# Two attention pairs transposed on TensorE, four output tiles in a borrowed buffer, one clear dropped, and later load estimates in a statically planned transformer kernel

## The chip, the cores and the metric

The kernel runs on one core of one Trainium2 chip. The metric is the device time of one execution in microseconds (us), the median of several executions. Each execution also reports its span (first to last instruction, about 1.7 us less than the device time) and the mean granted clock of TensorE, as a share of full speed. PE is TensorE, DVE is VectorE, ACT is ScalarE, POOL is GpSimd, SP is the engine that issues most DMAs.

## The reference, cut to what matters

Four layers follow each other on a sequence of 2048 tokens of width 640, in bf16: attention with a compressive memory, a feed-forward layer, then the same two again, each behind a layer norm and with a residual.

```python
x = x + A(layernorm(x))      # 32 heads of 20, 4 segments of 512 tokens
x = x + B(layernorm(x))      # relu(x @ w1) @ w2, inner width 1728
x = x + A(layernorm(x))
x = x + B(layernorm(x))
# A, per segment s: causal softmax attention inside the segment,
# and for s > 0 a read of the memory M, z that the earlier segments wrote
```

## The kernel before

The kernel does not issue instructions in the order of its source. Every stage is a generator that yields operations with an estimated cost; a list scheduler in the kernel orders them for the five engines and puts in semaphores. It does so 20 times, each time with due times worked out from the plan before, and emits the plan with the smallest estimated end:

```python
for n in range(PLANS):                      # PLANS = 20
    P, S = plan(dues)
    end = max(S.t.values())
    if best is None or end < best[0]:
        best = (end, P, S)
    dues = justify(S, dues, n)
```

Each engine gets its instructions in the planned order. Where an estimate is wrong, an instruction that is ready stands behind one that is not (3.67 us in the case near 305 us below). The planner also puts some useless "filler" matmuls on PE (`ps<-ident`, 50 in the kernel before).

The heads are laid out in groups of four, on partition rows 0-19, 32-51, 64-83 and 96-115. Three of the eight head groups (tile `kqL`) are made by a relay. In the first segment a set of selector matmuls does it; later segments go through DRAM:

```python
def relay_pe(a, s):                         # RELAY_PE = (0,): first segment only
    sel = hT[:, 0:128 * len(pieces)]...     # selectors, lent room in hT
    tz = yield dve(..., lambda e: e.memset(sel, 0.0))
    for i, (m, c, d0, d1) in enumerate(pieces):
        ... e.tensor_copy(selector slots, ident slots)        # seven small DVE copies
    # ... PE: matmul(bank, sel[:, i], kq chunk); evacuation to kqL[:, n, m, :], all 128 partitions
```

GpSimd clears `kqL` once at the start, and the relay waits for that:

```python
KQL[0].take()
def consts():
    # ...
    tl = yield pool(1600.0, lambda e: e.memset(kqL[:], 0.0))   # 3072 columns of bf16
    KQL[0].drop(tl)
    tm = yield pool(400.0, lambda e: e.memset(maskg[:], 0.0))
```

The results of an attention pair (two head groups) are evacuated (copied out of PE's result bank) to `oraw` and turned by one DMA transpose, then divided by the softmax sum on DVE:

```python
def turn(n, a, s, g, od, tk):
    # ... x == 0: evacuate to oraw[:, 0]; x == 1: to oraw[:, 1]
    tx, ok = yield XK(rw, [t0, te])                             # DMA transpose of the pair
    tr, rd = yield dve(240, 1, lambda e, d: e.reciprocal(d, ov[:, :, :, DH:E1]), [tx], [RDEN])
    # ... two products into o_sb
```

The output tiles of the first segment are then transposed on PE into two slots of `oT` (`OT`), and the output projection reads them.

The softmax here doesn't subtract the row's maximum and nothing guards it: scores larger than these inputs give would overflow.

Of the kernel before, what the change touches and what calls it, by code (L numbers as in the profile page):

```python
# [7 lines left out]
ACT = mybir.ActivationFunctionType  # L8
# [488 lines left out]
def bass_interleave_layers__memory_aug_infini_attn__dense_activation_relu__prompt_kernel(  # L497
    nc, A_x, A_wq, A_wk, A_wv, A_wo, A_beta, B_x, B_w1, B_w2, out,
):
    with contextlib.ExitStack() as es:  # L500
# [3 lines left out]
        def sem_(name):  # L504
            if name not in sems:
                sems[name] = es.enter_context(nc.semaphore(name))
            return sems[name]
# [4 lines left out]
        LN2_APART = (0, 7)  # L512

        LN1_PE, LN2_PE, OT_PE = (0, 1), (0,), (0,)
        HALVES = (0,)
        RELAY_PE = (0,)
        NXT, NXN, NET = 3, 2, 2
        wq_p = sb("wq_p", [128, FC, D])
        wk_p = sb("wk_p", [128, FC, D])
# [48 lines left out]
        def plan(dues):  # L568
# [22 lines left out]
            RMEM = [Slot(rmem[:, k], "rmem") for k in range(2)]  # L591
            OT = [Slot(oT[:, k], "oT") for k in range(2)]
            HT = [Slot(hT, "hT")]
            xnt_sem = [[sem_("xt%d_%d" % (k, i)) for i in range(NJ)] for k in range(NXT)]
            scw_sem = [[sem_("sw%d_%d" % (b, r)) for r in range(4)] for b in range(2)]
            scr_sem = [sem_("sr%d" % r) for r in range(4)]
# [14 lines left out]



            def ld(e, name, nbytes, fn, key, waits=(), issue=700.0, lat=2600.0):
                tk = yield dma(e, sem_("d_" + name), nbytes, fn, waits, issue=issue, lat=lat, rate=380.0)
                S.set(*key, v=[tk])
                return tk
# [93 lines left out]
                zb = yield dve(320, 1, lambda e: e.memset(w2_r[DFF - NFULL * 128:128, NFULL, :], 0.0))  # L711
                S.set("z1", v=[za, zb])

            KQL[0].take()

            def consts():
                t0 = yield pool(150, lambda e: e.memset(ident[:], 0.0))
                t1 = yield pool(230, lambda e: e.affine_select(
                    out=ident[:], in_=ident[:], compare_op=ALU.not_equal, fill=1.0, base=0,
                    pattern=[[-1, 128]], channel_multiplier=1), [t0])  # L720
                S.set("ident", v=[t1])
                S.fill = (lambda e, bank: e.matmul(bank[:, 0:128], ident[:], ident[:], start=True, stop=True), MISC, t1)
                tv0 = []
                for b in range(3):
                    tk = yield pool(100, lambda e, b=b: e.memset(v_flat[b][:, NJ * H * E1:NVA], 0.0))
                    tv0.append(tk)
                th = yield pool(150, lambda e: e.memset(nhalf[:], -0.5))
                S.set("nhalf", v=[th])
                tb = yield Need("beta")
                te = yield act(32, lambda e: e.activation(gt[:, 0, :], beta_bc[:], ACT.Exp), tb, psum=False)  # L730
                ta = yield act(32, lambda e: e.activation(gt[:, 1, :], gt[:, 0, :], ACT.Copy, bias=1.0), [te], psum=False)
                for b in range(3):
                    if b == 1:
                        yield Need("kq", 0, 0, 0)
                    o = v_aug[b][:, :, :, DH:E1]
                    i = gt[:, 1, :][:, None, :, None].to_broadcast([128, NJ, H, 1])
                    t = yield Op([("pool", 950.0, 60.0, one(lambda e, o=o, i=i: e.tensor_copy(o, i))),
                                  ("act", act_ns(128, False), 125.0, one(
                                      lambda e, o=o, i=i: e.activation(o, i, ACT.Copy)))], [ta])
                    S.set("one", b, v=[t, tv0[b]])  # L740
                tl = yield pool(1600.0, lambda e: e.memset(kqL[:], 0.0))
                KQL[0].drop(tl)
                tm = yield pool(400.0, lambda e: e.memset(maskg[:], 0.0))
                t1 = yield dve(32, 1, lambda e: e.tensor_scalar(
                    epsg[:].rearrange("p b (g r) o -> p (b g) r o", g=4),
                    gt[:, 1, :].rearrange("p (r g) -> p g r", r=4)[:, :, :, None], 1e-6, None, ALU.mult), [ta])
                S.set("epsg", v=[t1])
                tk = []
                for r in range(4):
                    p0 = 32 * r  # L750
                    t2 = yield dve(160, 1, lambda e, r=r, p0=p0: e.tensor_copy(
                        maskg[p0:p0 + DH, :, r, 0:DH],
                        gt[p0:p0 + DH, 0, 8 * r:8 * r + 8][:, :, None].to_broadcast([DH, G, DH])), [te, tm])
                    t3 = yield dve(8, 1, lambda e, r=r, p0=p0: e.memset(maskg[p0:p0 + DH, :, r, DH:E1], 1.0), [tm])
                    tk += [t2, t3]
                S.set("maskg", v=tk)
# [417 lines left out]
            def scores(m):  # L1174
# [71 lines left out]
                        bs.drop(tx)  # L1246
                        S.set("half", m, u, k, v=[tk, tx])

                if a * NSEG + s in HALVES:
                    for k in range(2):  # L1250
                        S.spawn(half(k), "scores")
                    for u in (0, 2):
                        yield from take(u)
                        S.set("taken", m, u > 1)
                    for u in range(5):
                        h0 = yield Need("half", m, u, 0)
                        h1 = yield Need("half", m, u, 1)
                        done(u, [h0[1], h1[1]])
                        ends(u, h0[0], h1[0])
                    return  # L1260
# [12 lines left out]
            def apply(n):  # L1273
                a, r = divmod(n, NSEG * G)
                s, g = divmod(r, G)
                b = room(a, s)
                mk = []
                for j in range(NJ):
                    tm = yield Need("p", n, j)
                    mk.append(tm)  # L1280
                pt = PTS[n % 2][0]
                vt = yield Need("v", a, s)
                va, vt = vt[0], vt[1:]
                x = n % 2

                def make(bank):
                    return [(lambda e, hh=hh, j=j: e.matmul(  # L1287
                        bank[32 * hh:32 * hh + 32, 128 * j:L],
                        v_flat[b][:, (j * H + 8 * hh + g) * E1:(j * H + 8 * hh + g) * E1 + 32],
                        PT[:, x, hh, PT_OFF[j]:PT_OFF[j] + L - 128 * j], start=(j == 0), stop=(j == NJ - 1)),  # L1290
                        j == NJ - 1 and hh == 3) for j in range(NJ) for hh in range(4)]

                o = pe(25.0 + 1280 / 2.4, make, mk + vt, [OD], mode="col")
                if a * NSEG + s in HALVES:
                    o.patience = 0.0
                tk, od = yield o
                pt.drop(tk)
                if g == G - 1:
                    va.drop(tk)
                S.spawn(turn(n, a, s, g, od, tk), "turn")  # L1300

            def turn(n, a, s, g, od, tk):

                x = n % 2
                if x == 0:
                    te, rw = yield evac(512, 1, lambda e, d: e.tensor_copy(d[:, 0, :], od.ap),
                                        lambda e, d: e.activation(d[:, 0, :], od.ap, ACT.Copy), [tk], [ORAW])
                    od.drop(te)
                    S.set("raw", n, v=[rw, te])
                    return  # L1310
# [29 lines left out]
                ok.drop(*to)  # L1340
                S.set("o", n - 1, v=[to[0]])
                S.set("o", n, v=[to[1]])

            class XK(Op):
                def __init__(self, rw, waits):
# [18 lines left out]
            def o_turn(a, s):  # L1364
# [6 lines left out]
                def by_pe(i):  # L1371
                    idt = yield Need("ident")

                    def make(bank):
                        return [(lambda e, c=c: e.transpose(
                            bf(bank)[:, c * 128:(c + 1) * 128], ob.ap[:, i, c * 128:(c + 1) * 128], ident[:]),
                            c == FC - 1) for c in range(FC)]
                    tT, bk = yield pe(56.0 * FC, make, ow + idt, [MISC])
                    ob.drop(tT)
                    src = bf(bk.ap)[:, 0:D]  # L1380
                    dst = lambda o: o.rearrange("p c t -> p (c t)")
                    tk, ot = yield evac(D, 1, lambda e, o: e.tensor_copy(dst(o), src),
                                        lambda e, o: e.activation(dst(o), src, ACT.Copy), [tT], [OT])
                    bk.drop(tk)
                    S.set("oT", a, s, i, v=[ot, tk])

                def by_xbar(i):
                    tk, ot = yield XT(i, ob, ow)
                    ob.drop(tk)
                    S.set("oT", a, s, i, v=[ot, tk])  # L1390

                for i in range(NJ):
                    if a * NSEG + s in OT_PE:
                        S.spawn(by_pe(i), "oturn")
                    else:
                        yield from by_xbar(i)
# [13 lines left out]
            def out_proj(a, s):  # L1410
                wt = yield Need("wo")
                for i in range(NJ):
                    t = 4 * s + i
                    ot, tc = yield Need("oT", a, s, i)
                    for hf in range(2):
# [10 lines left out]
                                    (lambda e: fn(e, bank), k == FC - 1)])  # L1426
                        S.spawn(add_half(t, hf, bk, tk, ("xA", a, s, i)), "oadd")
                    ot.drop(tk)

            def ln2(a, s):  # L1430
                def x_tks(i):
# [153 lines left out]
```

## Time and profile before

| | before |
|---|---|
| device time, median of 3 | 592.19 us (592.14 to 592.25) |
| span of the profiled execution, mean granted clock | 591.0 us, 0.994 |
| PE busy | 575.2 us, 97% |
| PE idle | 15.8 us |
| ACT / DVE / POOL busy | 427.3 / 425.9 / 215.5 us |

The page of the kernel before, its first two parts: busy time by engine, and the span in 40 slices of 14.8 us with the busy share in tenths. `PEclk` is the granted clock in tenths.

```profile
PE 575.2 (97%) x5086; PEld 297.3 (50%) x5086; DVE 425.9 (72%) x1018; ACT 427.3 (72%) x520; POOL 215.5 (36%) x342
PE   8989999999999899999999999999999999999998
...
PEclk9979999999999999999999999999999999999999
```

PE is the bound. There is one slice where the clock falls, the third. The table by stretches of the kernel before shows it closer; the columns are the stretch, its length, then busy time and instructions of PE, PE's weight loads, DVE, ACT and POOL, then the granted clock, the busy share of the DMA engines and GB/s.

```profile
31.00:32.00 1.00, 0.22 (x4) 0.05 (x1) 1.00 (x2) 1.00 (x3) 1.00 (x1) 1.00 0.00 0
32.00:33.00 1.00, 0.00 (x0) 0.00 (x0) 1.00 (x4) 1.00 (x2) 1.00 (x2) 1.00 0.00 0
33.00:34.00 1.00, 0.56 (x6) 0.41 (x7) 1.00 (x6) 0.09 (x1) 1.00 (x2) 1.00 0.00 0
34.00:35.00 1.00, 1.00 (x10) 0.15 (x8) 1.00 (x3) 0.00 (x0) 0.96 (x2) 0.66 0.82 97
35.00:36.00 1.00, 1.00 (x18) 0.44 (x16) 0.28 (x1) 0.90 (x1) 0.00 (x0) 0.50 0.75 282
...
40.00:41.00 1.00, 1.00 (x10) 0.27 (x10) 0.00 (x0) 0.63 (x2) 0.00 (x0) 0.50 0.95 185
41.00:42.00 1.00, 1.00 (x5) 0.39 (x4) 0.41 (x1) 1.00 (x2) 0.00 (x0) 0.93 1.16 216
```

PE idles for 2.2 us and then works at half speed for nearly 7 us, in which it loses about 3.4 us (the sum of one minus the clock). At half speed PE reads as 100% busy (1.00 in the rows from 35 to 41), so this loss is not idle time; the clock column shows it, and so does the length of the work: 16 matmuls of one form took 1.26 us at 34.99 and 0.73 us at 45.39. The timelines of POOL, DVE and PE around it, kernel before (start, duration, engine, line, what; in brackets the idle time just before it and who ended it):

```profile
30.14 2.65 POOL L741 MEMSET kqL<- 128x3072 bf16 x1
...
29.89 2.92 DVE L989 COPY hT<-ident 128x48 bf16<-128x48 bf16 x3
30.23 2.76 DVE L826 TENSOR_SCALAR xn_tok<-x_sb,mv,rstd 128x640 bf16<-128x640 bf16 x1
...
33.04 0.45 PE L790 MATMUL ps<-ident,xn_tok 128*128 128x128 bf16 x5 [1.82 <-DVE xn_tok L826]
33.90 0.62 PE L1011 MATMUL ps<-wb,hT 128*128 128x512 bf16 x2 [0.40 <-DVE oraw L1306]
```

The clear ends at 32.79. Two DVE instructions that began near 30 end at 32.81 and 32.99. The same normalise takes 0.4 to 0.9 us elsewhere in this trace (0.94 once, at 24.26). Here the instruction took 2.76 us and ended 0.2 us after the clear.

### The profile page before, as it was taken

The page shows a single profiled execution, that of the slowest core. Times are in us where ns is not written, and L with a number is a line of the kernel's source. Part 1 is how long each engine was busy: PE and PEld are TensorE (multiplying, and loading weights), DVE is VectorE, ACT ScalarE, POOL GpSimd, SP SyncE. Part 2 cuts the span into 40 slices and gives each one's busy share as a digit, 9 for nine tenths or more (in the row PEclk, how much of TensorE's full clock was granted, in tenths as well). Part 3 has the DMA queues.
Part 4 walks back from the last instruction along what each step waited for, and adds up shares of the span by engine and source line. Part 5 has one row for each costly group of instructions (what it writes and reads, how often), then busy time and mean ns, then how long its engine had stood idle before and what let it go on. Part 6 is the DMA issues. An engine that isn't in the chain of part 4 may idle for free.

```text
span 591.0 us, 12433 instructions
## 1 busy us (share of the span) xinstructions
PE 575.2 (97%) x5086; PEld 297.3 (50%) x5086; DVE 425.9 (72%) x1018; ACT 427.3 (72%) x520; POOL 215.5 (36%) x342
## 2 busy tenths in 40 slices
PE   8989999999999899999999999999999999999998
PEld 4423345434565354564444555455544654655655
DVE  6769769999979974899755985597827898734202
ACT  4869999989888888878787776897787787123140
POOL 4556644745343543344433440344322333002000
PEclk9979999999999999999999999999999999999999
DMA  6244593494743531256329314254408451331201
GB/s 211 91 110 102 101 166 66 57 216 95 106 84 70 110 64 37 41 109 118 63 32 150 52 26 88 43 94 89 68 2 105 101 92 31 84 69 23 68 0 45
DMA packets 126609, 48.44 MB, mean 82 GB/s; under 512 B 114056, under 2 KB 125256, under 8 KB 126552
## 3 DMA queue, kind: packets, MB, share of 16 engines
q1 hardware_dynamic: 124600, 40.10, 38.2%
q0 software_dynamic: 1520, 7.21, 4.0%
q8 instruction: 40, 0.66, 0.4%
q10 hardware_dynamic: 432, 0.34, 0.2%
q14 instruction: 17, 0.14, 0.1%
HBM read 13.77 MB, written 6.06 MB: 34 GB/s over the span
## 4 chain that ended last, share of the span: by engine, by line
PE 76%; DVE 13%; ACT 6%; DMA 3%; issue 1%; POOL 0%; SPq 0%
PE ps L1486 20%; PE ps L1466 16%; PE ps L878 13%; PE ps L1418 7%; PE ps L1205 7%; PE ps L1287 6%; PE ps L912 5%; ACT PT L1219 4%; DMA wb<-in_A_wk_dram 2%; DVE hT L1449 1%; ACT PT L1216 1%; DVE xn_tok L826 1%; DVE o_sb L1336 1%; PE ps L1155 1%; DMA oT<-o_sb 1%; DVE o_sb L1144 1%
## 5 line engine op out<-in xcount | busy, mean ns | idle before, releaser
L1219 ACT ACTIVATE PT<-ps 128x1024 bf16<-128x1024 f32 x256 | 248.3, 1031 | 49.9 <-PE ps L1205 49.1
L1195 POOL TENSOR_SCALAR_AFFINE_SELECT PT<-PT 128x512 bf16<-128x512 bf16 x256 | 172.2, 689 | 266.3 <-ACT PT L1219 220.1
L1466 PE MATMUL ps<-xnT,wb 128*128 128x512 bf16 x560 | 135.4, 380 | 3.0 <-DVE hT L1449 3.0
L1486 PE MATMUL ps<-wb,hT 128*128 128x320 bf16 x896 | 131.9, 299 | 0.6 <-DVE o_sb L1144 0.5
L1360 DVE TENSOR_TENSOR x_sb<-x_sb,ps 128x320 bf16<-128x320 bf16 x128 | 60.9, 479 | 69.8 <-PE ps L1486 53.4
L1486 PEld LDWEIGHTS ps<-wb,hT 128*128 128x128 bf16 x896 | 83.5, 98 | 39.6 <-issue 7.8
L1466 PEld LDWEIGHTS ps<-xnT,wb 128*128 128x128 bf16 x560 | 50.5, 98 | 63.5 <-issue 7.6
L1450 ACT ACTIVATE hT<-ps 128x512 bf16<-128x512 f32 x54 | 32.3, 598 | 56.8 <-PE ps L1466 56.5
L1216 ACT ACTIVATE PT<-ps 128x1024 bf16<-128x1024 f32 x64 | 62.2, 1028 | 10.9 <-PE ps L1205 10.7
L912 PE MATMUL ps<-wv_r,xnT 128*128 128x320 bf16 x320 | 60.3, 300 | 1.5 <-DVE va L900 0.6
L865 DVE CAST kq<-ps 128x512 bf16<-128x512 f32 x44 | 30.1, 686 | 36.4 <-PE ps L878 36.4
L878 PE MATMUL ps<-xnT,wk_p 128*128 128x512 bf16 x200 | 55.3, 381 | 0.0
L878 PE MATMUL ps<-xnT,wq_p 128*128 128x512 bf16 x200 | 54.8, 386 | 0.1
L1418 PE MATMUL ps<-wo_r,oT 128*128 128x320 bf16 x320 | 52.6, 300 | 1.2 <-DMA oT<-o_sb 0.9
L1449 DVE TENSOR_SCALAR hT<-ps 128x512 bf16<-128x512 f32 x58 | 39.4, 681 | 8.2 <-PE ps L1466 7.7
L912 PEld LDWEIGHTS ps<-wv_r,xnT 128*128 128x128 bf16 x320 | 29.6, 98 | 23.0 <-issue 3.9
L1287 PE MATMUL ps<-PT,va 128*32 128x128 bf16 (+3 forms) x896 | 40.7, 302 | 0.0
L826 DVE TENSOR_SCALAR xn_tok<-x_sb,mv,rstd 128x640 bf16<-128x640 bf16 x64 | 37.0, 590 | 4.8 <-DMA xnT<-xn_tok 3.6
L1418 PEld LDWEIGHTS ps<-wo_r,oT 128*128 128x128 bf16 x320 | 29.7, 98 | 18.6 <-issue 3.8
L1205 PE MATMUL ps<-kq 20*128 20x512 bf16 (+3 forms) x560 | 35.3, 301 | 0.1
L813 DVE BATCH_NORM_STATS2 stats<-x_sb 128x6 f32<-128x320 bf16 x64 | 29.7, 465 | 2.8 <-DMA x_sb<-in_A_x_dram 2.5
L1287 PEld LDWEIGHTS ps<-PT,va 128*32 128x32 bf16 x896 | 18.9, 96 | 23.7 <-issue 11.2
(100 smaller groups left out, 617.7 us busy)
## 6 DMA issues: line engine op xcount, KB each, us to landing
kq_scr<-kq SPq DMA_DIRECT2D x28, 120.0 KB
kqL<-kq_scr SPq DMA_DIRECT2D x28, 120.0 KB
out_dram<-x_sb SPq DMA_DIRECT2D x16, 160.0 KB, 1.8
wb<-in_B_w_dram POOLq DMA_DIRECT2D x5, 432.0 KB, 3.5
x_sb<-in_A_x_dram POOLq DMA_DIRECT2D x3, 640.0 KB, 5.5
wb<-in_B_w_dram POOLq DMA_DIRECT2D x2, 640.0 KB, 6.9
xnT<-xn_tok SPq DMA_TRANSPOSE x52, 2.7
wv_r<-in_A_wv_dram SPq DMA_DIRECT2D x1, 800.0 KB, 7.2
```

Of the source, the lines that this page charges most:

```text
L878: fn = lambda e, bank, k=k, w_p=w_p, c=c: e.matmul(bank, w_p[:, k, c * 128:(c + 1) * 128], xnT[:, k_, :, k, :], start=(k == 0), stop=(k == ...
L912: fn = lambda e, bank, k=k, i=i, hf=hf: e.matmul(bank[:, 0:320], xnT[:, k_, i, k, :], wv_r[:, k, hf * 320:(hf + 1) * 320], start=(k == 0), ...
L1195: tm = yield pool(590.0, lambda e: e.affine_select(out=reg, in_=reg, pattern=[[0, 4], [1, 128]], compare_op=ALU.is_ge, fill=0.0, base=0, c ...
L1205: fns.append((lambda e, x=x, j=j, hh=hh, N=N, o=o: e.matmul(ps[:, hh, o:o + N], kq(b, gg[x], 0)[32 * hh:32 * hh + DH, 128 * j:128 * j + 12 ...
L1216: fn = lambda e: e.activation(PT[:, :, 2 * k:2 * k + 2, 1024:1280], bs.ap.rearrange("p h (x t) -> p x h t", x=2), ACT.Exp, scale=SCALE)
L1219: fn = lambda e: e.activation(PT[:, items[0], 2 * k:2 * k + 2, c0:c0 + 512], bs.ap, ACT.Exp, scale=SCALE)
L1287: return [(lambda e, hh=hh, j=j: e.matmul(bank[32 * hh:32 * hh + 32, 128 * j:L], v_flat[b][:, (j * H + 8 * hh + g) * E1:(j * H + 8 * hh + ...
L1360: ta = yield dve(320, 1, lambda e: e.tensor_tensor(xa, xa, bk.ap[:, 0:320], ALU.add), [tk], early=HOT)
L1418: fn = lambda e, bank, k=k, hf=hf, o=ot.ap: e.matmul(bank[:, 0:320], o[:, k, :], wo_r[:, k, hf * 320:(hf + 1) * 320], start=(k == 0), stop ...
L1449: th = yield evac(512, 1, lambda e: e.tensor_scalar(hTv[:, dc, :], bk.ap, 0.0, None, ALU.max), lambda e: e.activation(hTv[:, dc, :], bk.ap ...
L1466: fn = lambda e, bank, k=k, dc=dc: e.matmul(bank, w1_r[:, k, dc * 128:(dc + 1) * 128], xnT[:, k_, :, k, :], start=(k == 0), stop=(k == FC ...
L1486: fn = lambda e, bank, dc=dc, i=i, hf=hf: e.matmul(bank[:, 0:320], hTv[:, dc, i * 128:(i + 1) * 128], w2_r[:, dc, hf * 320:(hf + 1) * 320] ...
```

## The change

Its intent: pairs 2 and 3 of the first segment reach `o_sb` without the DMA transpose; the output transposes need not wait for one of two slots; the clear goes, since the relay's matmuls of the first segment write every partition of `kqL` anyway; and the plan expects the first weights 1.7 us later.

```diff
-        HALVES = (0,)
+        HALVES = (0, 1, 2, 3)          # with the tests below: the same pairs as before
+        TURN_PE = (2, 3)
+            OTB = [Slot(hT[:, k * D:(k + 1) * D].rearrange("p (c t) -> p c t", c=FC), "oTb") for k in range(NJ)]
-            def ld(e, name, nbytes, fn, key, waits=(), issue=700.0, lat=2600.0):
+            def ld(e, name, nbytes, fn, key, waits=(), issue=700.0, lat=4300.0):
-            KQL[0].take()
-                tl = yield pool(1600.0, lambda e: e.memset(kqL[:], 0.0))
-                KQL[0].drop(tl)
-                if a * NSEG + s in HALVES:
+                if m in HALVES:                    # likewise n // 2 in apply()
+                if n // 2 in TURN_PE:
+                    yield from turn_pe(n, a, s, g, od, tk)
+                    return
+            def turn_pe(n, a, s, g, od, tk):
+                # ... evacuate to oraw as before, then
+                def make(bank):
+                    return [(lambda e, i=i: e.transpose(
+                        bf(bank)[:, i * 128:(i + 1) * 128], rw.ap[:, x, i * 128:(i + 1) * 128], ident[:]),
+                        i == NJ - 1) for i in range(NJ)]
+                tT, bk = yield pe(56.0 * NJ, make, [te] + idt, [MISC])
+                # ... reciprocal and product read the PSUM bank directly
-                    # by_pe(i): evacuation into          [tT], [OT])
+                    # by_pe(i): evacuation into          [tT] + HT[0].old, [OTB])
+                if a * NSEG + s in OT_PE:
+                    yield Op([("sp", 0.0, 0.0, lambda: [])], [], users=NJ, hold=[HT[0]])
+                    if a * NSEG + s in OT_PE:      # at the end of each tile in out_proj
+                        HT[0].drop(tk)
```

One thing is not in the diff: any of these edits makes the scheduler plan all 590 us anew.

More of the change, by code (lines that the diff above doesn't have):

```diff
@@ L1293, in apply @@
                 o = pe(25.0 + 1280 / 2.4, make, mk + vt, [OD], mode="col")
-                if a * NSEG + s in HALVES:
+                if n // 2 in HALVES:
                     o.patience = 0.0
@@ L1342, in turn @@
                 S.set("o", n, v=[to[1]])
+            def turn_pe(n, a, s, g, od, tk):
+                x = n % 2
+                if x == 0:
+                    te, rw = yield evac(512, 1, lambda e, d: e.tensor_copy(d[:, 0, :], od.ap),
+                                        lambda e, d: e.activation(d[:, 0, :], od.ap, ACT.Copy), [tk], [ORAW], users=2)
+                    S.set("raw", n, v=[rw])
+                else:
+                    rw, = yield Need("raw", n - 1)
+                    te = yield evac(512, 1, lambda e: e.tensor_copy(rw.ap[:, 1, :], od.ap),
+                                    lambda e: e.activation(rw.ap[:, 1, :], od.ap, ACT.Copy), [tk] + rw.old)
+                od.drop(te)
+                idt = yield Need("ident")
+                def make(bank):
[3 more added lines that the diff above has]
+                tT, bk = yield pe(56.0 * NJ, make, [te] + idt, [MISC])
+                rw.drop(tT)
+                ov = bf(bk.ap)[:, 0:512].rearrange("p (i r e) -> p i r e", i=NJ, r=4)
+                tr, rd = yield dve(120, 1, lambda e, d: e.reciprocal(d[:, 0:NJ], ov[:, :, :, DH:E1]), [tT], [RDEN], early=HOT)
+                ob = yield Need("ob", a, s)
+                to = yield dve(320, 1, lambda e: e.tensor_tensor(
+                    ob.ap.rearrange("p i (r g e) -> p i r g e", r=4, g=G)[:, :, :, g, :], ov[:, :, :, 0:DH],
+                    rd.ap[:, 0:NJ].to_broadcast([128, NJ, 4, DH]), ALU.mult), [tr] + ob.old, early=HOT)
+                bk.drop(to)
+                rd.drop(to)
+                S.set("o", n, v=[to])
             class XK(Op):
@@ L1382, in by_pe @@
                     tk, ot = yield evac(D, 1, lambda e, o: e.tensor_copy(dst(o), src),
-                                        lambda e, o: e.activation(dst(o), src, ACT.Copy), [tT], [OT])
+                                        lambda e, o: e.activation(dst(o), src, ACT.Copy), [tT] + HT[0].old, [OTB])
                     bk.drop(tk)
```

## The prediction

> **What bounds it now.** TensorE. The page gives PE 575.2 us busy of 591.0 (97%); PE is 76% of the chain that ended last. PE is idle for 15.8 us, of which about 1.25 us before the first warm-up matmul and 2.9 us after the last one. A change can win only from the other 11.6 us, from time at a reduced clock, and from filler matmuls.
>
> **The one expensive place.** In the table by stretches, PE is busy 0.22 us of 31-32, 0 of 32-33, 0.56 of 33-34, and the granted clock is then 0.66 in 34-35, 0.50 from 35 to 41 and 0.93 in 41-42: 2.2 us of idle time plus about 3.4 us lost to the half clock (sum of one minus the clock). The timeline shows the cause: GpSimd clears kqL at 30.14 for 2.65 us. Beside it, on VectorE, the 128x640 normalise takes 2.76 us (0.4 to 0.8 elsewhere) and the first three selector copies 2.92 us; both end when the clear ends. PE waits 1.82 us for that xn_tok, and 0.40 us at 33.90. [...] here 6.8 us of half clock follow the gap.
>
> **What the change does.**
> 1. Drops the kqL clear. The relay matmuls of the first segment write every partition of kqL anyway. I expect the copies to fall to their normal lengths, the 1.8 us gap to shrink to under 0.5 us and the clock to stay at 1.00: -5.0 us (1.8 idle, 3.2 clock), straight on PE's path.
> 2. Pairs 2 and 3 of segment 0 leave the DMA transpose. Adds 16 transposes of 128x128 at about 56 ns (five take 0.28 us of PE's stream): +0.9 us of PE. Now the last pair's transpose is issued at 73.33, its reciprocal runs only at 83.45, its products end at 85.2, and the first output transpose runs at 90.4. Without the DMA, products should be done near 76, and output projection and second layer norm of segment 0 start up to 10 us sooner.
> 3. Four output tiles in hT's room instead of two: no waiting for a slot. VectorE, 97-100% busy from 100 to 130, gets layer norm work off earlier (49% busy in 80-90). PE idles 2.9 us in 80-130 and 1.7 us in 160-200; I expect to win 1.5 us.
> 4. Weights taken as 1.7 us later in the plan: no data arrives sooner (wk lands at 11.1, wq at 13.1). PE idles only 0.44 us in 10-20, so at most 0.4 us. The rewritten HALVES condition selects the same pairs: 0.
>
> Sum: -5.0 + 0.9 - 1.5 - 0.4 = -6.0 us, all of it on PE, so it should reach the end. Replanning moves later stages by a microsecond either way.
>
> **Prediction.** 586.2 us, 8 in 10 between 582.5 and 590.5. Faster by over 2%: 0.05; within 2%: 0.93; slower by over 2%: 0.02.
>
> **What would show it.** (1) No clear of kqL; normalise near 30 us under 1 us; granted clock 1.00 in 30-42. (2) PE busy near 572; 16 PE transposes from oraw; 30 DMA transposes of oraw instead of 32. (3) Output projection of segment 0 starting before 88; PE idle in 80-130 under 2 us.
>
> **What would make it wrong.** A gap of over 1.5 us elsewhere in 28-45 (affine selects, selector copies still waiting on GpSimd), so that the half clock comes back: then about 590. A new long wait where PE's in-order stream meets an evacuated oraw tile. Or a new plan that also closes late gaps: then below 583.

The "over 1.5 us" of its last paragraph is the author's estimate; the trace shows one gap, waits of 1.82 and 0.40 us, with half clock after it.

## The result, and the profile after

| | before | after |
|---|---|---|
| device time | 592.22 us (592.14 to 593.39, 4 runs) | 589.24 us (588.61 to 589.36, 4 runs) |
| span, granted clock of the profiled execution | 591.0 us, 0.994 | 587.4 us, 0.999 |
| PE busy | 575.2 us | 572.9 us |
| PE idle | 15.8 us | 14.5 us |

The ratio is 0.9943, with a 95% interval of 0.9926 to 0.9960. Ratios are the mean time of one kernel's fast runs over that of the other's of the same rounds, so not quite the ratio of the medians quoted. The verdict is "same" at 2%, with a gain of 3.0 us where 6.0 was predicted.

The page of the changed kernel, the same lines:

```profile
PE 572.9 (98%) x5104; PEld 298.6 (51%) x5104; DVE 419.4 (71%) x1010; ACT 432.2 (74%) x530; POOL 211.5 (36%) x341
PE   8999999999999999999989999999999999999998
...
PEclk9999999999999999999999999999999999999999
```

The low slice of the clock is gone, and one weaker slice of PE has appeared in the middle, the 21st. The waits of the changed kernel by stretch of time, from PE's timeline: first the only one left between 30 and 45 us, then the longest of the later ones.

```profile
32.62 0.39 PE L1205 MATMUL ps<-wb 20*128 20x384 bf16 x4 [0.60 <-ACT PT L1219]
...
241.16 0.72 PE L1523 MATMUL ps<-wb,hT 128*128 128x320 bf16 x4 [0.97 <-DVE hT L1486]
...
307.67 0.60 PE L1503 MATMUL ps<-xnT,wb 128*128 128x512 bf16 x2 [2.06 <-DVE hT L1486]
...
395.21 0.84 PE L1453 MATMUL ps<-wo_r,oT 128*128 128x320 bf16 x5 [0.90 <-DVE x_sb L1393]
```

POOL and DVE at the place of the former clear, changed kernel; the granted clock is 1.00 throughout 30-45. The seven selector copies now run at 1.8 to 2.4 us, at 0.16 to 0.18 us each:

```profile
31.59 0.73 POOL L743 MEMSET maskg<- 128x672 bf16 x1
...
30.16 0.45 DVE L826 TENSOR_SCALAR xn_tok<-x_sb,mv,rstd 128x640 bf16<-128x640 bf16 x1 [0.40 <-POOL rstd L822]
...
31.74 0.76 DVE L826 TENSOR_SCALAR xn_tok<-x_sb,mv,rstd 128x640 bf16<-128x640 bf16 x1 [0.37 <-POOL rstd L822]
```

The second normalise stands beside the mask's memset, which ends at 32.32, and ends 0.2 us after it.

The balance of PE, worked out from the tables by stretches of the two profiled executions (idle is the length of the stretch less PE's busy time; 130-550 is the sum of five stretches):

| stretch, us | idle before | idle after | difference |
|---|---|---|---|
| 0-30 | 1.74 | 1.60 | -0.1 |
| 30-45 | 2.22 | 0.62 | -1.6 |
| 45-130 | 3.99 | 2.08 | -1.9 |
| 130-550 | 4.93 | 7.38 | +2.5 |
| 550-end | 2.87 | 2.80 | -0.1 |
| busy time | 575.25 | 572.91 | -2.3 |
| span | 591.0 | 587.4 | -3.6 |

Busy time fell by 2.3 us: about 3.4 us of the half clock less 0.9 us estimated for the 16 new transposes (from the 0.28 us that five take), to within 0.2 us. So the early gain is there as predicted, and 2.5 us of it come back as idle time after 130 us, in stages whose operations the change does not touch.

The 2.06 us wait at 307.67 shows what such a late gap is made of. DVE's timeline and the DMA issues of the changed kernel just before it:

```profile
298.40 3.47 SPq L1386 DMA_TRANSPOSE otok<-oraw  x1
...
305.70 0.35 DVE L1321 RECIPROCAL rden<-otok 128x32 f32<-128x32 bf16 x1 [3.67 <-DMA otok<-oraw]
306.09 0.93 DVE L1329 TENSOR_TENSOR o_sb<-otok,rden 128x320 bf16<-128x320 bf16 x1
306.94 0.68 DVE L1486 TENSOR_SCALAR hT<-ps 128x512 bf16<-128x512 f32 x1
```

The plan had put the reciprocal of a pair ahead of an evacuation. The pair's DMA transpose, issued at 298.40, let DVE go only at 305.70, 7.3 us later; the median landing of these transposes is 3.2 us in this trace. DVE stood still for 3.67 us with the evacuation behind the reciprocal, and PE waited for the bank that the evacuation would free. The profile names "DVE hT" as the releaser; the cause is one step further back, a DMA.

### The profile page after: what moved, and what is told of

It reads as the page before. It is cut to its first block, busy times and chain, and to the rows that moved or that the text cites. A ratio compares the mean times of both kernels' runs of the same rounds, so it can differ in the third digit from the quotient of the medians.

```text
span 587.4 us, 12468 instructions
## 1 busy us (share of the span) xinstructions
PE 572.9 (98%) x5104; PEld 298.6 (51%) x5104; DVE 419.4 (71%) x1010; ACT 432.2 (74%) x530; POOL 211.5 (36%) x341
## 4 chain that ended last, share of the span: by engine, by line
PE 72%; DVE 18%; ACT 6%; DMA 2%; issue 1%; POOL 1%; DVEq 0%
PE ps L1523 18%; PE ps L1503 15%; PE ps L878 11%; PE ps L1453 7%; PE ps L1205 6%; PE ps L912 6%; PE ps L1287 5%; ACT PT L1219 3%; DVE hT L1486 2%; DVE xn_tok L826 2%; DMA otok<-oraw 1%; ACT PT L1216 1%; DVE phq L1125 1%; DVE otok L1334 1%; DVE o_sb L1144 1%
## 5 line engine op out<-in xcount | busy, mean ns | idle before, releaser
L1195 POOL TENSOR_SCALAR_AFFINE_SELECT PT<-PT 128x512 bf16<-128x512 bf16 x256 | 169.6, 679 | 269.9 <-ACT PT L1219 220.1
L1523 PE MATMUL ps<-wb,hT 128*128 128x320 bf16 x896 | 134.0, 300 | 2.3 <-DVE hT L1486 1.2
L1487 ACT ACTIVATE hT<-ps 128x512 bf16<-128x512 f32 x59 | 35.2, 599 | 54.9 <-PE ps L1503 54.5
L878 PE MATMUL ps<-xnT,wk_p 128*128 128x512 bf16 x200 | 53.3, 380 | 0.1
L1453 PE MATMUL ps<-wo_r,oT 128*128 128x320 bf16 x280 | 45.9, 300 | 0.9 <-DVE x_sb L1393 0.9
L1486 DVE TENSOR_SCALAR hT<-ps 128x512 bf16<-128x512 f32 x53 | 36.1, 682 | 12.3 <-PE ps L1503 12.1
L826 DVE TENSOR_SCALAR xn_tok<-x_sb,mv,rstd 128x640 bf16<-128x640 bf16 x64 | 33.3, 537 | 6.5 <-POOL rstd L822 4.1
L1453 PEld LDWEIGHTS ps<-wo_r,oT 128*128 128x128 bf16 x280 | 25.8, 98 | 16.9 <-issue 4.9
```

The lines of the kernel that those rows point to most:

```text
L878: fn = lambda e, bank, k=k, w_p=w_p, c=c: e.matmul(bank, w_p[:, k, c * 128:(c + 1) * 128], xnT[:, k_, :, k, :], start=(k == 0), stop=(k == ...
L1195: tm = yield pool(590.0, lambda e: e.affine_select(out=reg, in_=reg, pattern=[[0, 4], [1, 128]], compare_op=ALU.is_ge, fill=0.0, base=0, c ...
L1453: fn = lambda e, bank, k=k, hf=hf, o=ot.ap: e.matmul(bank[:, 0:320], o[:, k, :], wo_r[:, k, hf * 320:(hf + 1) * 320], start=(k == 0), stop ...
L1486: th = yield evac(512, 1, lambda e: e.tensor_scalar(hTv[:, dc, :], bk.ap, 0.0, None, ALU.max), lambda e: e.activation(hTv[:, dc, :], bk.ap ...
L1523: fn = lambda e, bank, dc=dc, i=i, hf=hf: e.matmul(bank[:, 0:320], hTv[:, dc, i * 128:(i + 1) * 128], w2_r[:, dc, hf * 320:(hf + 1) * 320] ...
```

## The experiments

Twelve runs were made, each with the kernel before on the same chip. Two theories were held against each other.

- Theory A: the clear on GpSimd is the early loss, by the delay and by the clock; the missing 3 us were lost to the draw of a new plan.
- Rivals: (B) the clear is a bystander and the new early order won the time; (C) the late gaps belong to what turned pairs and shared room displace.

"Frozen plan" means that the scheduler saw exactly the same operations and costs, so that the instructions of every engine stand in the same order, apart from the edit itself. The traces bear this out: the instruction lists of each engine are the same in all four frozen runs, apart from the edit.

### The clear alone, plan frozen

```diff
-                tl = yield pool(1600.0, lambda e: e.memset(kqL[:], 0.0))
+                tl = yield pool(1600.0, lambda e: e.memset(kqL[:, 0, 0, 0:16], 0.0))
```

> The kernel before with its plan frozen (same instructions in the same order on every engine); only the clear of kqL writes 16 columns instead of 3072. Theory A (the clear blocks VectorE, that makes the idle stretch at 31-34 us and the half clock after it): 587.2 us, within 0.8, idle of PE in 30-45 under 0.7 us, clock 1.00 there. Rival B (the early gain of the changed kernel came from the new order at the start, weights later and pairs turned on PE; the clear is a bystander): 591 to 592.2, gap and half clock still there.

Measured: 587.87 us (586.68 to 588.32, 4 runs), clock 1.000 in all four; before on this chip 591.02 (589.08 to 592.45, 7 runs); ratio 0.9944 (0.9918 to 0.9971). PE idles 0.45 us in 30-45. DVE's copies and normalise, and PE's largest wait there:

```profile
29.79 0.38 DVE L989 COPY hT<-ident 128x48 bf16<-128x48 bf16 x3
30.11 1.05 DVE L826 TENSOR_SCALAR xn_tok<-x_sb,mv,rstd 128x640 bf16<-128x640 bf16 x1
...
32.01 0.59 PE L1011 MATMUL ps<-wb,hT 128*128 128x512 bf16 x2 [0.33 <-DVE hT L989]
```

The three copies fall from 2.92 to 0.38 us, the normalise from 2.76 to 1.05; why it is not shorter was not looked into. The outcome is A's. One argument of one memset gives as much as the whole change did. Rival B falls.

### Half of the clear, plan frozen

```diff
-                tl = yield pool(1600.0, lambda e: e.memset(kqL[:], 0.0))
+                tl = yield pool(1600.0, lambda e: e.memset(kqL[:, 0], 0.0))
```

> Same frozen plan, the clear cut to 1536 columns (about 1.33 us). Theory A [...]: VectorE is let go about 1.3 us sooner, PE idles 0.9 us or less, the clock stays at 1.00, so about 588 us, most of the gain of the 16-column clear. If the clock instead falls in proportion to the gap: about 589.7. Rival B: 591 to 592.2.

Measured: 587.83 us (587.35 to 588.83, 4 runs), clock 1.000 in all four. The half clear takes 1.38 us, and PE's two waits are 0.54 and 0.40 us where they were 1.82 and 0.40. So the clock did not fall in proportion to the gap: it did not fall at all.

```profile
30.43 1.38 POOL L741 MEMSET kqL<- 128x1536 bf16 x1
...
30.52 1.48 DVE L826 TENSOR_SCALAR xn_tok<-x_sb,mv,rstd 128x640 bf16<-128x640 bf16 x1
...
32.06 0.45 PE L790 MATMUL ps<-ident,xn_tok 128*128 128x128 bf16 x5 [0.54 <-DVE xn_tok L826]
```

The normalise again ends about when the clear does, 0.2 us after it. With a clear of 2.65 us it took 2.76, with 1.38 us 1.48: it is held for the length of the clear.

### A clear put into the changed kernel, plan frozen

```diff
-                tm = yield pool(400.0, lambda e: e.memset(maskg[:], 0.0))
+                tm = yield Op([("pool", 400.0, 60.0, lambda: [(lambda e: e.memset(xnT[:, 2], 0.0), False),
+                     (lambda e: e.memset(oT[:, 0, 0:4], 0.0), False), (lambda e: e.memset(maskg[:], 0.0), True)])], [])
```

> The changed kernel with its plan frozen, and a clear of 3072 columns (two memsets of tiles that nobody uses yet) put in front of the mask's memset on GpSimd, at about 31.6 us, not planned for. Theory A: VectorE is held up to 2.6 us behind the 128x640 normalise at 31.7 us; PE gets a gap of 1 to 2 us in 32-36; 590 us if the clock holds, 593 to 594 if it falls. Rival B: within 0.6 us of the changed kernel, 588.6 to 589.8.

Measured: 592.60 us (591.28 to 595.57, 4 runs). By execution: 591.46 at clock 1.000, 595.57 at 0.991, 591.28 at 1.000, 593.74 at 0.994. So 2 us over the changed kernel at full clock, and 4 to 6 us where the clock fell. The direction fits A; at full clock the time is 1.4 us above the 590 that A named, and the place is another one. The normalise was held for 3.41 us, to 35.11: not to the end of the clear (34.31) but to that of the mask's memset behind it (34.91). But PE's gap came later than expected, at 37-39 us, when an evacuation of `kqL` behind it on DVE was late:

```profile
31.54 2.30 POOL L743 MEMSET xnT<- 128x2560 bf16 x1
33.72 0.59 POOL L743 MEMSET oT<- 128x512 bf16 x1
34.18 0.73 POOL L743 MEMSET maskg<- 128x672 bf16 x1
...
31.70 3.41 DVE L826 TENSOR_SCALAR xn_tok<-x_sb,mv,rstd 128x640 bf16<-128x640 bf16 x1
...
39.30 0.31 PE L912 MATMUL ps<-wv_r,xnT 128*128 128x320 bf16 x1 [2.06 <-DVE kqL L994]
```

With this gap in the program, the clock fell in two of four executions. The profiled one kept it, so where it fell in the others was not seen.

### The clear taken out of the plan, nothing else changed

```diff
-            KQL[0].take()
-                tl = yield pool(1600.0, lambda e: e.memset(kqL[:], 0.0))
-                KQL[0].drop(tl)
```

> The kernel before with the clear taken out of the plan, so that everything is planned anew; the rest of the change left out. The planner gives its best plan 583.8 us where it gave the kernel before and the changed kernel 579.4. Theory A plus a planner whose numbers carry over: no gap at 31 us, -5 us, but +4.4 us of new gaps later: about 591.5. If the planner's numbers say nothing: about 587. Rival B: 592 or more.

Measured: 593.01 us (591.99 to 593.90, 4 runs), 5 us over the frozen plan with the 16-column clear, though the operations are the same but for that clear and 14 more filler matmuls. The time lies in the range named for rival B, but the trace speaks against B: the early gap is gone (0.46 us idle in 30-45, clock 1.00), while PE idles 5.8 us in 45-130 instead of 4.0, and 7.0 us in 130-550 instead of 5.0. The gain was eaten by the new plan. The plans' estimated ends, 583.8 us against 579.4, had said about that much. The clocks were 1.000, 0.997, 0.999 and 0.994 for 593.90, 593.81, 592.21 and 591.99 us: here the clock fell without the clear, and it does not sort the times.

### PE's gap filled with useless matmuls, plan frozen, full clear kept

```diff
             fns = make(*[s.ap for s in got])
             # ...
+            if getattr(op, "prefill", 0):
+                fn_, _, after_ = self.fill                 # ident x ident
+                self.P.waits(e, [t for s in got for t in s.old] + [after_])
+                for k in range(op.prefill):
+                    self.P.op("pe", lambda e, ap_=got[0].ap: fn_(e, ap_), False)
             self.P.waits(e, waits)
             # ... at the transposes of the normalised tiles:
-                        tT, bk = yield pe(56.0 * FC, make, [tn] + idt, [MISC])
+                        o = pe(56.0 * FC, make, [tn] + idt, [MISC])
+                        if f == 0 and s == 1 and i == 3:
+                            o.prefill = 24
+                        tT, bk = yield o
```

> The kernel before, plan frozen, the full clear kept; 24 filler matmuls (about 1.3 us at full clock) stand in PE's stream where it waited 1.82 us for the fourth normalised tile. This takes away the idleness but not the delay. Theory A: the clear costs about 1.3 to 2 us by the delay [...]; filled, every execution keeps the clock at 1.000 and takes about 589.1 us, as the one execution of the kernel before at clock 1.000 did (589.08), still 1.3 us over the kernel with the 16-column clear. Rival: the clock falls for another reason than PE's idleness; then clocks of 0.994 to 0.997 come back and the median is 591 as before.

Measured: 589.26 us (588.70 to 589.90, 4 runs), clock 1.000 in all four. The kernel before had 1.000, 0.997, 0.994, 1.000, 0.994, 0.997 and 0.997. The clear, and PE's timeline:

```profile
29.67 2.65 POOL L746 MEMSET kqL<- 128x3072 bf16 x1
...
30.58 1.50 PE L727 MATMUL ps<-ident 128*128 128x128 bf16 x24
32.57 0.45 PE L795 MATMUL ps<-ident,xn_tok 128*128 128x128 bf16 x5 [0.49 <-DVE xn_tok L834]
33.42 0.59 PE L1019 MATMUL ps<-wb,hT 128*128 128x512 bf16 x2 [0.40 <-DVE oraw L1314]
```

This separates the two costs of the clear. The delay alone costs 589.26 - 587.87 = 1.4 us (two chips); on the chip of the 16-column clear, the one execution of the kernel before at full clock gives 589.08 - 587.87 = 1.2 us. The rest, which only some executions meet, is the clock. The 21 executions of the kernel before sort themselves by their granted clock:

| granted clock | executions | device time, us |
|---|---|---|
| 1.000 | 3 | 589.02 to 589.17 |
| 0.997 | 11 | 590.17 to 591.56 |
| 0.994 | 7 | 591.50 to 592.91 |

One step of 0.003 is 1.8 us of 590. To lose 1.8 us at a clock of 0.50 takes about 3.5 us, an estimate from these numbers. The profiled execution, at 0.994, shows 6.8 us of half clock, about twice that. No execution of this kernel at 0.997 was profiled, so its half clock was not seen, and what puts an execution into one of the three groups was not shown by a run. The clock is not the only source of spread: the run with seed 1 below had the full clock in all four executions and took 587.62 to 589.72 us.

### The same operations, another draw of the plan

```diff
-            dues = justify(S, dues, n)
+            rnd = random.Random(49 * 1000 + n)              # seed 49, or 1
+            dues = {k: v + rnd.gauss(0.0, 50) for k, v in justify(S, dues, n).items()}
```

Nothing but the order is touched, and with it the number of filler matmuls (52 in the changed kernel and with seed 49, 67 with seed 1): the due times that rank the operations get a random shift of 50 ns. Seed 49 was chosen among 86 draws for its low estimated end and seed 1 for its high one.

> The changed kernel, the same operations; the due times that order the plan get a random jitter of 50 ns (seed 49). The planner gives its best plan 578.2 us against 579.4 for the changed kernel. Theory A (the missing 3 us are a draw of the plan: late gaps of PE that the planner places by chance, and its own numbers carry over to the chip): about 588.0 us, faster than the changed kernel. Rival C (the late gaps belong to the change, by what turned pairs and shared room displace): 589.2, within 0.6, whatever the draw.

> As the run before, with seed 1: the planner gives its best plan 582.1 us, the worst of 86 draws (mean 580.1, standard deviation 0.7). Theory A: about 592 us, with new idle stretches of PE. Rival C: 589.2 within 0.6.

Measured: seed 49 took 586.29 us (585.40 to 587.73, 4 runs), ratio to before 0.9919 (0.9887 to 0.9950). Seed 1 took 588.20 us (587.62 to 589.72, 4 runs), ratio 0.9960 (0.9930 to 0.9989). Half of A's expectation missed: seed 1 was to take 592 us and took 588.2, less than the changed kernel. So the draw moves the time by some 3 us, but the estimated end (578.2, 579.4 and 582.1 us for seed 49, the changed kernel and seed 1) does not rank the draws reliably. PE's idle time in 130-550, in profiled executions, was 6.3 us for seed 49 and 4.4 us for seed 1, against 7.4 us in the changed kernel and 4.9 us in the kernel before. Rival C would have this idle time fixed by the change; it is not. But idle time alone does not rank the draws: the two profiled executions took about the same time (587.73 and 587.62 us), with PE busy for 570.6 us with seed 49 and for 574.3 with seed 1.

### Parts of the change undone, each planned anew

Without pairs on PE:

```diff
-        TURN_PE = (2, 3)
+        TURN_PE = ()
```

> The changed kernel with no pair turned on PE (pairs 2 and 3 of the first segment go through the DMA transpose again), planned anew: the planner gives 581.7 us. Theory A: 589.2 + 2.3 = 591.5 us; PE does 0.9 us less, output projection of segment 0 starts some 10 us later, PE idles 4 us instead of 2 us in 45-130. Rival C: the turned pairs cost, so 588 or less.

Measured: 593.38 us (591.15 to 593.88, 4 runs) with clocks of 0.994, 0.997, 0.997 and 1.000; the one at full clock took 591.15. PE idles 4.3 us in 45-130 against 2.1 with the pairs turned, as A expected. The fall of the clock was not expected. In the profiled execution, at 0.994, the half clock lies at 107-115 us (mean clock 0.96 over 45-130), after two waits that have nothing to do with a clear:

```profile
104.89 0.33 PE L1155 MATMUL ps<-BD,phq 128*128 128x84 bf16 x4 [1.05 <-DVE xnT L797]
107.75 0.61 PE L1205 MATMUL ps<-kqL 20*128 20x256 bf16 x8 [0.83 <-ACT PT L1219]
```

With the output tiles in two slots:

```diff
-                    # ... [tT] + HT[0].old, [OTB])
+                    # ... [tT], [OT])
-                if a * NSEG + s in OT_PE:
-                    yield Op([("sp", 0.0, 0.0, lambda: [])], [], users=NJ, hold=[HT[0]])
-                    if a * NSEG + s in OT_PE:
-                        HT[0].drop(tk)
```

> The changed kernel with its output tiles back in the two slots of oT instead of four in hT's room, planned anew (planner: 584.1 us). If four slots matter: output transposes of segment 0 wait for slots, PE idle in 45-130 goes from 2 us to over 3.5 us, 591 us or more. If the two slots were enough: only the draw differs, 587 to 590, idle in 45-130 near 2 us.

Measured: 591.31 us (590.63 to 591.41, 4 runs); PE idles 3.3 us in 45-130. The time is what was expected if the slots matter; the idle time fell just short of the 3.5 us named.

With the loads expected early again:

```diff
-            def ld(e, name, nbytes, fn, key, waits=(), issue=700.0, lat=4300.0):
+            def ld(e, name, nbytes, fn, key, waits=(), issue=700.0, lat=2600.0):
```

> The changed kernel with the first weights expected 1.7 us sooner in the plan again, as before (planner: 581.4 us). If the later estimate matters at the start: PE idle in 0-30 rises by about 0.5 us and the early order shifts, 590 us. If not: 0-30 as in the changed kernel, and the total anywhere in 587 to 590 by the draw of the plan.

Measured: 588.10 us (587.88 to 589.14, 4 runs), 1.1 us less than the changed kernel beside it. PE waits once for 2.0 us for the weights of v and idles 4.2 us in 0-30 instead of 1.7, and still the whole is no slower.

```profile
PE ps L912 <- DMA wv_r<-in_A_wv_dram: 2.0, 1, 2.0
```

Neither expectation fits: the idle time rose by more than the 0.5 us named, and the time fell. The later estimate does what it should at the start, and that start is worth nothing by the end in this pair of plans.

Each of these three is a single draw of a plan, and draws of the unaltered operations lay between 586.2 and 589.2. The first two lie 2 us or more above all three draws of the changed kernel, which speaks for turned pairs and four slots; three draws are too few to call their sizes shown.

### The changed kernel and the better draw on one chip

> The changed kernel itself, unaltered, to have it on the same chip as the three others of this call. 589.2 us within 0.8, clock 0.999 to 1.000; it should equal those executions of the kernel before that keep the full clock (589.0 to 589.2 on two chips so far).

> The draw with 50 ns jitter, seed 49, once more beside the changed kernel. If the plan's draw matters: 586.3 within 0.8, 2 to 3 us under the changed kernel on the same chip, with no overlap of the runs. If the difference came from the chip: equal within 0.8.

Measured: the changed kernel 589.20 us (589.00 to 590.56), the draw with seed 49 586.16 us (585.13 to 588.47), four runs each with no overlap; before 591.45 us (590.17 to 592.91, 7 runs). The ratios to before are 0.9965 (0.9944 to 0.9986) and 0.9914 (0.9886 to 0.9943). The seeded draw is the fastest kernel: 3 us under the changed kernel with the same operations. PE idles 5.8 us in 130-550 there against 7.5 us in the changed kernel beside it, and is busy for 571.3 us against 572.7. One execution of each ran at a clock of 0.997, and was the slowest of its four: the changed kernel too can lose some clock.

## Why the prediction was right or wrong

The measured 589.24 us lies in the range (582.5 to 590.5) and the class, within 2%, was the most likely one. The gain was half of the point estimate, 3.0 us of 6.0. Step by step:

1. "-5.0 us (1.8 idle, 3.2 clock), straight on PE's path": right in mechanism, and right in size for an execution at a clock of 0.994. The normalise fell from 2.76 to 0.45 and 0.76 us, PE's idle time in 30-45 from 2.2 to 0.6 us, and the clock stayed at 1.00 there in the profiled execution. The selector copies did not merely get shorter, as predicted: the new plan also moved them to the start. With the plan frozen the profiled span fell from 591.0 to 586.1 us, 4.9 us. What the prediction did not see is that the clock's share is a chance: of the 21 later executions of the kernel before, 3 kept the full clock. The delay alone was worth 1.2 to 1.4 us, not 1.8.
2. "+0.9 us of PE" and "up to 10 us sooner": 16 transposes and 30 instead of 32 DMA transposes are there, and the output projection of segment 0 starts at 79.4 us instead of 94.5. Undoing it, with a new plan, cost 2 us at full clock.
3. "I expect to win 1.5 us" from idle time in 80-130 and 160-200: the idle time in 80-130 fell from 2.9 to 1.7 us (in 45-130 by 1.9 us), that in 160-200 stayed at 1.7, and the gain did not reach the end.
4. "At most 0.4 us" for the later loads: idle time in 0-30 fell by 0.1 us. Undone, with a new plan, the kernel was 1.1 us faster.
5. "Replanning moves later stages by a microsecond either way": this is the term that failed. Idle time after 130 us grew by 2.5 us, and draws of the plan for the very same operations took 586.2, 588.2 and 589.2 us. The error of the sum, 3.0 us, is mostly this term; 0.4 to 0.6 us of the delay in step 1 is another part.

Put together, the kernel before at full clock takes 589.0 to 589.2 us, and the changed kernel 589.2 us. Its whole measured gain is as large as the loss at half clock, which it mostly removed; the rest of what it won early was given back late. That it was given back by the draw of the plan is supported by the seeded kernels, which remove part of it with no change of the operations. Which later gap each early edit caused, and how far turned pairs and four slots help on average over plans, stays open. The kernel before was not redrawn, so whether its own plan was a lucky draw is open too.

## What to carry to other kernels

Look at the granted clock beside the busy share: PE at half speed looked 100% busy here, and a gap of about 2 us cost another 1.7 to 4.2 us in the executions whose clock fell (18 of 21 of the kernel before, 2 of 4 of the changed kernel with a clear put in) and nothing in the others, so sort the executions by their clock before comparing medians. Where a kernel is planned by a heuristic, test an edit once with the plan frozen, to get its own effect, and compare re-planned versions only over several random draws. A large clear on GpSimd is not free because GpSimd is idle: here a normalise on VectorE took 2.76 us beside a clear of 2.65, and 1.05 in the frozen plan when the clear wrote 16 columns. Ask which VectorE instructions run beside it and who waits for those.
